# Pair 0 of x by SyncE alone: backward mirrored loads in the order of use, Q later, g_ln turned by TensorE

## Chip, cores and metric

The kernel runs on one core of a Trainium2 chip. The metric is the device time of one execution in microseconds. Before the change the median of three runs is 1128.04 us (1126.84 to 1128.88).

## What is computed

```python
X = np.fft.fft(x, axis=1)          # x: 8 x 3136 x 256, float32
X = np.fft.fft(X, axis=2)
t = X.real.reshape(25088, 256)
h = t @ w_in                       # 256 x 1024, float64
e = np.exp(h - h.max(-1))
s = h * e / (e.sum(-1) + 1e-09)
ln = (s - s.mean(-1)) / np.sqrt(s.var(-1) + 1e-06) * g_ln
out = ln @ w_out                   # 1024 x 256
```

The result is float32. The tables of the transforms (F, T, Q) and of row numbers (mirror) are inputs of the program.

## The kernel before

The batch is taken in four pairs of two images. In an image the 3136 rows are written as 49 x 64, n = 64 n1 + n2, so that a pair has 2 x 49 = 98 partitions, each with 64 rows of x. The real part of the transform needs rows n and -n only as a sum (features reversed too). Of the 64 columns, 32 are therefore loaded forward (`xa`, columns 1 to 32) and their mirror partners as `xb`; they come in NC = 8 chunks of CH = 4 rows (98 x 4096 bytes each). The mirror partners of the partitions of one image are its partitions in reverse, read from the last columns backward.

`load` (line 118) issues one chunk: `xa` from SyncE's queue (126), `xb` from GpSimd as an indirect DMA (128) whose row numbers are in `idx`, and with the last chunk `x0`, column 0. `add_mirror` (137) adds `xb` to `xa` in place, two VectorE instructions (143 and 145); `fold` (153) makes sums and differences of the features with lines 150, 151 and 163, into `y` (two buffers). `transform1` (185) multiplies a half chunk of `y` with F on TensorE (215), copies the result out on ScalarE (218), and `keep` (222) stores it to `zd` in DRAM (223), first only the 20 rows that the first group of frequencies needs. `turn` (225) reads `zd` back in another order for the second transform.

`Weights` (637) works beside this for pair 0. `w_in` comes as float64 bits in four pieces of 128 x 4096 bytes (`piece_in`, 581), and VectorE and ScalarE make float32 of them (`exponent_in`, `narrow_in`: lines 584 to 634). `Q` (664) is multiplied into the weights by `product_in` (685), `mid` (672) spreads one column of Q on ScalarE (676). `w_out` comes in two halves (700) and is made float32 and scaled by `g_ln` in `exponent_out` and `narrow_out`; `scale_out` (703) multiplies `g_ln` by 2**-20 first. `g_ln` is loaded by line 665 into 128 x 8, element by element.

The order of all this is written out by hand (`manual_schedule`, 784): each engine executes its instructions in the order in which they are written. SyncE's queue at the start is `idx`, w_in 0, w_in 1, xa 0, F, w_in 2, xa 1, w_in 3, xa 2, xa 3, Q, g_ln, xa 4, xa 5, then, as chunks are done, xa 6 and so on. The mirrored halves 0 to 5 stand on GpSimd at once. A SyncE DMA signals one of eight semaphores in turn, and its issue waits until the DMA eight places before it has landed. Chunks 2 to 5 lie in `room`, memory that is later `uT`; chunks 6 and 7 use the buffers of 0 and 1 again. For each chunk VectorE has: a piece of w_in (chunks 0 to 2), `add_mirror`, `fold`; after chunk 7 it goes on with w_out. In the turn of chunk 3, before its `transform1`, stand the loads of w_out and of T, `mid` and `scale_out`; after it `product_in(0)`.

From then on one unit (pair, k1) follows the other: second transform, products with w_in, softmax and statistics, products with w_out, store. Pairs 1 to 3 are loaded and folded beside the units, with GpSimd's indirect DMA for the mirrored half, and pair 0's outputs use `idx` too.

Of the kernel before, what the change touches and what calls it, by code (L numbers as in the profile page):

```python
# [9 lines left out]
FP32 = mybir.dt.float32  # L10
# [7 lines left out]
P = 128  # L18


N1, N2 = 49, 64
NK = N1 // 2 + 1
NH = N2 // 2
PR = 2 * N1
ZR = 4 * NK
CH = 4
NC = NH // CH
# [17 lines left out]
def kernel(  # L45
# [19 lines left out]
    nc = tc.nc  # L65
    B, S, D = x.shape
    FF = moe_w_in.shape[1]
    KF = FF // P
# [2 lines left out]
    HW = FF // 2  # L71

    x_g = x.rearrange("b (n1 g l) d -> (b n1 g) (l d)", n1=N1, l=CH)
    x_pn = x.rearrange("b (n1 n2) d -> (b n1) n2 d", n2=N2)
    out_k = out.rearrange("(p k2 k1) d -> p k1 k2 d", p=NP, k1=N1)

# [8 lines left out]
    fpool = ctx.enter_context(tc.tile_pool(name="fpool", bufs=2))  # L85
# [3 lines left out]
    F = const.tile([PR, 6, ZR], FP32, name="F")  # L89
# [6 lines left out]
    ident = const.tile([P, P], FP32, name="ident")  # L96
    neg_half = const.tile([P, 2], FP32, name="neg_half")
    idx = const.tile([P, NP * (NC + NK)], I32, name="idx")
    w_mid = const.tile([P, FF], FP32, name="w_mid")
    g_ln = const.tile([P, KF], FP32, name="g_ln")  # L100
# [5 lines left out]
    def result(i):  # L106

        return banks[i % 4]
# [9 lines left out]
    def load(pr, c, room=None):  # L118

        r = slice(pr.p * PR, (pr.p + 1) * PR)  # L120
        if room is None:
            xa = xpool.tile([PR, CH, D], FP32, tag="xa", name="xa")
            xb = xpool.tile([PR, CH, D], FP32, tag="xb", name="xb")
        else:
            xa, xb = (t.rearrange("p (l d) -> p l d", d=D) for t in room)
        nc.sync.dma_start(out=xa, in_=x_pn[r, c * CH + 1 : (c + 1) * CH + 1, :])
        i = pr.p * NC + c
        nc.gpsimd.indirect_dma_start(
            out=xb.rearrange("p l d -> p (l d)"), out_offset=None, in_=x_g,
            in_offset=bass.IndirectOffsetOnAxis(ap=idx[0:PR, i : i + 1], axis=0))  # L130
        x0 = None
        if c == NC - 1:
            x0 = xpool.tile([PR, 1, D], FP32, tag="x0", name="x0", bufs=1)
            nc.sync.dma_start(out=x0, in_=x_pn[r, 0:1, :])
        pr.raw[c] = (xa, xb, x0)

    def add_mirror(pr, c, engine, part=None):

        xa, xb, _ = pr.raw[c]
        rows = (0, CH) if part is None else (part * CH // 2, (part + 1) * CH // 2)  # L140
        r = slice(rows[0], min(rows[1], CH - 1 if c == NC - 1 else CH))
        a, rb = xa[:, r, :], xb[:, ::-1, :][:, r, :]
        i = engine.tensor_tensor(out=a[:, :, 1:D], in0=a[:, :, 1:D], in1=rb[:, :, D - 1 : 0 : -1], op=ALU.add)
        if part is None:
            engine.tensor_tensor(out=a[:, :, 0:1], in0=a[:, :, 0:1], in1=rb[:, :, 0:1], op=ALU.add)
        return i
# [6 lines left out]
    def fold(pr, c):  # L153

        xa, _, x0 = pr.raw.pop(c)
        pr.y[c] = xpool.tile([PR, CH, D], FP32, tag="y", name="y")
        sides = [(pr.y[c], xa)]
        if c == NC - 1:
            pr.y0 = xpool.tile([PR, 1, D], FP32, tag="y0", name="y0", bufs=1)
            sides.append((pr.y0, x0))  # L160
        for o, i in sides:
            fold_features(o, i)
            nc.vector.tensor_copy(out=o[:, :, 0:129:128], in_=i[:, :, 0:129:128])  # L163
# [21 lines left out]
    def transform1(pr, s):  # L185

        c, l = divmod(2 * s, CH)
        if s == 0:  # L190
            pr.zd = dram.tile([ZR, NH, D], FP32, tag="zd", name="zd")
        if l == 0:

            if pr.p or c < 2:
                pr.z = zpool.tile([ZR, CH, D], FP32, tag="z", name="z")
            elif c < 6:
                if c == 2:
                    pr.z_v = fpool.tile([P, 2, FF, 2], FP32, tag="v", name="z_v", bufs=2)
                pr.z = pr.z_v[0:ZR].rearrange("p a f b -> p (a f b)").rearrange("p (c l d) -> p c l d", c=4, l=CH)[:, c - 2]
            elif c == 6:  # L200
                pr.z = S_tiles[1][0:ZR, 0:2].rearrange("p a c k -> p (a c k)").rearrange("p (l d) -> p l d", l=CH)
            else:
                pr.z = gpool.tile([P, KG, D], FP32, tag="g", name="z_g")[0:ZR, 0:CH, :]
            pr.zs[c] = pr.z
        y = pr.y[c]
        ps = result(0 if pr.p else s).rearrange("p (l d) -> p l d", l=2)
        if s == NH // 2 - 1:
            parts = [(ps[0:ZR, 0], y[:, l], 0), (ps[0:ZR, 1], pr.y0[:, 0], 1), (ps[0:ZR, 1], y[:, l + 1], 2)]
        else:
            parts = [(ps[0:ZR], y[:, l : l + 2], 0)]  # L210
        pr.done.append(s)
        first = True
        for o, i, t in parts:
            for h, cs in enumerate((EVEN, ODD)):
                nc.tensor.matmul(o[..., cs], F[:, 2 * t + h, :], i[..., cs], start=first, stop=True,  # L215
                                 skip_group_check=True)
                first = False
        nc.scalar.copy(pr.z[:, l : l + 2, :], ps[0:ZR])
        if l == CH - 2:
            keep(pr, c, slice(0, ZR if pr.p else 4 * KG))  # L220
# [375 lines left out]
    def confine(unit, here=False, parts=(0, 1, 2)):  # L596

        if unit is None:
            return
        if here:  # L600
            bits(unit, unit, -896.0, ALU.add, 0.0, ALU.max)
            bits(unit, unit, 255.0, ALU.min, 2.0 ** 23, ALU.mult)
            return

        u = unit.bitcast(FP32)
        for i in parts:
            if i == 0:
                nc.scalar.activation(out=u, in_=unit, func=ACT.Relu, bias=limits[:, 0:1])
            elif i == 1:
                nc.scalar.activation(out=u, in_=u, func=ACT.Relu, bias=limits[:, 1:2], scale=-1.0)  # L610
            else:
                nc.scalar.activation(out=unit, in_=u, func=ACT.Identity, bias=limits[:, 2:3], scale=-(2.0 ** 23))
# [24 lines left out]
    class Weights:  # L637
# [24 lines left out]
        def load_tables(self):  # L662
            self.Q = fpool.tile([P, KD, D + 1], FP32, tag="ev", name="Q", bufs=1)
            nc.sync.dma_start(out=self.Q, in_=q_tab.rearrange("(c p) d -> p c d", p=P))
            nc.sync.dma_start(out=g_ln, in_=moe_g_ln.rearrange("(c p) -> p c", p=P))

        def load_table(self, i):
            k1 = slice(KG, NK) if i else slice(0, KG)
# [32 lines left out]
                                  in_=moe_w_out.bitcast(I32).rearrange("(c p) f -> p c f", p=P)[:, c])  # L701

        def scale_out(self):
            nc.scalar.mul(out=g_ln, in_=g_ln, mul=2.0 ** -20)

        def exponent_out(self, i):
            self.units.append(exponent(moe_w_out, self.raw[:, 2 * i * NW : 2 * (i + 1) * NW]))
# [76 lines left out]
    with tc.manual_schedule():  # L784
        pairs = [Pair(p) for p in range(NP)]
        first, weights = pairs[0], Weights()
        nc.sync.dma_start(out=idx, in_=mirror)
        make_identity(nc, ident)

        rooms = {}  # L790
# [2 lines left out]
            room = room[0:PR].rearrange("p w c i m -> p (w c i m)").rearrange("p (a n) -> p a n", a=4)  # L793
            rooms[c], rooms[c + 1] = [room[:, i] for i in (0, 1)], [room[:, i] for i in (2, 3)]
        weights.load_in()
        for c in range(4):
            weights.piece_in(c)
            if c:
                load(first, c - 1, rooms.get(c - 1))
            if c == 1:  # L800
                nc.sync.dma_start(out=F, in_=f_tab)
        load(first, 3, rooms[3])
        weights.load_tables()
        for c in range(4, 6):
            load(first, c, rooms[c])
        nc.vector.memset(ones, 1.0)
        nc.vector.memset(neg_half, -0.5)
        bits(top_bit, neg_half[:, 0:1].bitcast(I32), 31, ALU.logical_shift_right, 31, ALU.logical_shift_left)
# [6 lines left out]
        for c in range(NC):  # L815

            if c == 0:
                weights.narrow_in(0)
                weights.narrow_in(1)
            elif c < 3:  # L820
                weights.narrow_in(c + 1)
            if c < 2:
                weights.exponent_in(c + 2)
            add_mirror(first, c, nc.vector)
            fold(first, c)
            if c == NC - 1:
                for i in range(2):
                    weights.exponent_out(i)
                confine(weights.units[0], True)
                weights.narrow_out(0)  # L830
            if c + 6 < NC:
                load(first, c + 6)
            if c == 3:
                weights.place_out()
                for i in range(2):
                    weights.load_out(i)
                weights.load_table(0)
                weights.mid()
                weights.scale_out()
            for s in range(CH // 2):  # L840
                if c == NC - 1:
                    confine(weights.units[0], parts=(s,))
                transform1(first, c * CH // 2 + s)
            if c == 3:
                weights.keep_in(0, weights.product_in(0))
            elif c == 4:
                odd = weights.product_in(1, (0,))
            elif c == 5:
                weights.product_in(1, (1,), odd)
# [312 lines left out]
```

## Time and profile before

| | us |
|---|---|
| median of 3 runs | 1128.04 |
| the profiled execution | 1129.0 |
| its span | 1127.1 |
| PE busy | 1092.4 (97%) |
| DVE busy | 986.5 (88%) |
| ACT busy | 799.4 (71%) |
| POOL busy | 809.9 (72%) |
| SyncE's DMA queue, share of 16 engines | 63.7% |
| GpSimd's DMA queue, share of 16 engines | 13.3% |

Read it so: PE is TensorE's matmuls, DVE VectorE, ACT ScalarE, POOL GpSimd, SP SyncE. A busy time is summed over the span. In the page's strips each digit is the busy share, in tenths, of one fortieth of the span (28.2 us). A row of the timeline has the start, the duration, the engine, the line, the operation with its operands, and in brackets how long the engine stood idle before it and what ended that. An "SPq" row is the issue of a DMA and not its transfer. The trace also records the packets of the DMA engines with their size and duration, and each increment of a DMA semaphore: every DMA engine that takes part in a transfer posts one when its share has landed.

### The profile page before, as it was taken

The page shows a single profiled execution, that of the slowest core. Times are in us where ns is not written, and L with a number is a line of the kernel's source. Part 1 is how long each engine was busy: PE and PEld are TensorE (multiplying, and loading weights), DVE is VectorE, ACT ScalarE, POOL GpSimd, SP SyncE. Part 2 cuts the span into 40 slices and gives each one's busy share as a digit, 9 for nine tenths or more (in the row PEclk, how much of TensorE's full clock was granted, in tenths as well). Part 3 has the DMA queues.
Part 4 walks back from the last instruction along what each step waited for, and adds up shares of the span by engine and source line. Part 5 has one row for each costly group of instructions (what it writes and reads, how often), then busy time and mean ns, then how long its engine had stood idle before and what let it go on. Part 6 is the DMA issues. An engine that isn't in the chain of part 4 may idle for free. (4 is left out here: it accounts for less than half of the span.)

```text
span 1127.1 us, 21958 instructions
## 1 busy us (share of the span) xinstructions
PE 1092.4 (97%) x7030; PEld 873.9 (78%) x7030; DVE 986.5 (88%) x1440; ACT 799.4 (71%) x1946; POOL 809.9 (72%) x707
## 2 busy tenths in 40 slices
PE   2999999999999999999999999999999999999997
PEld 1657878878777787887887787887877788778887
DVE  7899898988889989898888989898888899898984
ACT  4579777777766877777767777777776777777761
POOL 3058888766896988775877788876686576766674
PEclk9899999999999999999999999999999999999999
DMA  9773897867897989976969797976779685965665
GB/s 239 215 198 85 179 198 189 175 151 152 152 196 154 194 178 193 183 154 142 169 151 184 169 194 177 203 176 150 154 147 169 131 164 116 162 141 114 140 136 120
DMA packets 458569, 185.77 MB, mean 165 GB/s; under 512 B 425774, under 2 KB 440374, under 8 KB 458456
## 3 DMA queue, kind: packets, MB, share of 16 engines
q1 hardware_dynamic: 444568, 145.96, 63.7%
q0 software_dynamic: 13888, 38.42, 13.3%
q8 instruction: 57, 0.93, 0.4%
q14 instruction: 56, 0.46, 0.1%
HBM read 44.78 MB, written 38.80 MB: 74 GB/s over the span
## 5 line engine op out<-in xcount | busy, mean ns | idle before, releaser
L279 PE MATMUL ps_h<-Wi,q 128*128 128x512 f32 x800 | 361.9, 593 | 2.2 <-DVE nmax L300 2.0
L455 POOL TENSOR_TENSOR S<-uT 128x512 f32<-128x512 f32 x186 | 238.5, 1282 | 111.0 <-DVE u L315 37.4
L462 PE MATMUL ps_m<-Ws,S 128*128 128x128 f32 x2304 | 296.3, 275 | 2.8 <-POOL rs L377 2.8
L462 PEld LDWEIGHTS ps_m<-Ws,S 128*128 128x128 f32 x2304 | 279.8, 192 | 6.3 <-POOL rs L377 2.9
L322 ACT ACTIVATE h<-u,usum 128x1024 f32<-128x1024 f32 x196 | 225.0, 1149 | 78.2 <-DVE u L315 76.9
L279 PEld LDWEIGHTS ps_h<-Wi,q 128*128 128x128 f32 x800 | 144.1, 190 | 147.1 <-issue 141.4
L315 DVE SCALAR_TENSOR_TENSOR u<-h,u 128x1024 f32<-128x1024 f32 x196 | 236.7, 1243 | 7.7 <-ACT u L308 7.7
L308 ACT ACTIVATE u<-h,nmax 128x1024 f32<-128x1024 f32 x196 | 223.4, 1141 | 4.6 <-DVE nmax L300 2.9
L386 DVE STREAM_TRANSPOSE v<-u 128x2048 f32<-128x2048 f32 x88 | 203.4, 2311 | 3.0
L462 PE MATMUL ps_m<-Wo,uT 128*128 128x128 f32 x1536 | 203.7, 276 | 1.0 <-DMA out_dram<-ot 1.0
L462 PEld LDWEIGHTS ps_m<-Wo,uT 128*128 128x128 f32 x1536 | 187.9, 192 | 2.1 <-issue 2.1
L549 POOL DMA_INDIRECT out_dram<-ot,idx x96 | 112.7, 1174 | 35.0 <-issue 12.6
L300 DVE CUSTOM_DVE_ANT_0 h<-ev,ps_h 128x1024 f32<-128x1024 f32 x100 | 122.1, 1221 | 17.4 <-DVE ev L292 9.0
L300 DVE CUSTOM_DVE_ANT_0 h<-h,ps_h 128x1024 f32<-128x1024 f32 x96 | 117.2, 1221 | 14.6 <-ACT ot L506 1.0
L292 DVE SCALAR_TENSOR_TENSOR ev<-w_mid,r,ps_h 128x1024 f32<-128x1024 f32 x99 | 122.9, 1241 | 1.4 <-PE ps_h L279 1.0
L455 POOL TENSOR_TENSOR S<-uT,S 128x512 f32<-128x512 f32 x93 | 118.9, 1279 | 7.2
L455 POOL TENSOR_TENSOR S<-S,uT 128x512 f32<-128x512 f32 x93 | 118.9, 1278 | 7.3
L462 PE MATMUL ps_m<-Ws,uT 128*128 128x128 f32 x768 | 101.8, 276 | 0.0
L462 PE MATMUL ps_m<-Wo,S 128*128 128x128 f32 x768 | 101.4, 275 | 0.0
L243 PEld LDWEIGHTS ps_m<-T,g 128*128 128x128 f32 x400 | 60.1, 191 | 47.3 <-issue 45.7
L215 PE MATMUL ps_m<-y,F 98*100 98x258 f32 (+3 forms) x288 | 72.0, 385 | 22.6 <-DVE y L163 22.6
L462 PEld LDWEIGHTS ps_m<-Ws,uT 128*128 128x128 f32 x768 | 93.8, 192 | 0.0
(109 smaller groups left out, 1186.6 us busy)
## 6 DMA issues: line engine op xcount, KB each, us to landing
uT<-v SPq DMA_DIRECT2D x752, 128.0 KB
g<-zd POOLq DMA_DIRECT2D x72, 160.0 KB, 5.4
out_dram<-ot SPq DMA_DIRECT2D x176, 64.0 KB
xa<-in_x_dram SPq DMA_DIRECT2D x28, 392.0 KB
zd<-z SPq DMA_DIRECT2D x24, 400.0 KB
raw_in<-in_moe_w_in_dram SPq DMA_DIRECT2D x4, 512.0 KB
raw_out<-in_moe_w_out_dram SPq DMA_DIRECT2D x2, 1024.0 KB
room<-in_x_dram SPq DMA_DIRECT2D x4, 392.0 KB
```

Of the source, the lines that this page charges most:

```text
L215: nc.tensor.matmul(o[..., cs], F[:, 2 * t + h, :], i[..., cs], start=first, stop=True, skip_group_check=True)
L243: nc.tensor.matmul(o, g[:, k, h * P : (h + 1) * P], table, start=(h == 0), stop=True, skip_group_check=True)
L279: nc.tensor.matmul(ps[:, fs], t.q[:, c * P : (c + 1) * P], Wi[:, c, fs], start=True, stop=not whole_even)
L292: nc.vector.scalar_tensor_tensor(out=t.ev, in0=w_mid, scalar=t.r, in1=ps, op0=ALU.mult, op1=ALU.add)
L300: nc.vector.tensor_tensor_reduce(out=t.h[s], in0=t.h[0] if s else t.ev, in1=t.odd, scale=1.0 if s else -0.5, scalar=3.0e38, op0=ALU.add, o ...
L308: nc.scalar.activation(out=t.u[s], in_=t.h[s], func=ACT.Exp, bias=t.nmax[:, s : s + 1], scale=-1.0, accum_out=t.esum[:, s : s + 1])
L315: t.last = nc.vector.scalar_tensor_tensor(out=t.u[s], in0=t.h[s], scalar=-1.0, in1=t.u[s], op0=ALU.mult, op1=ALU.mult, accum_out=t.usum[:, ...
L322: nc.scalar.activation(out=t.h[s], in_=t.u[s], func=ACT.Square, bias=t.usum[:, s : s + 1], scale=-float(FF), accum_out=t.ssq[:, s : s + 1])
L386: nc.vector.transpose(out=t.batch.v[:, :, t.w], in_=t.both.rearrange("p s (g n) -> p (s g) n", n=32))
L455: i = engine.tensor_tensor(out=S[j], in0=a, in1=b, op=op)
L462: nc.tensor.matmul(o, a[:, c], b[:, c], start=start and c == 0, stop=c == n - 1, skip_group_check=True)
L549: dma = nc.gpsimd.indirect_dma_start(out=out, out_offset=bass.IndirectOffsetOnAxis(ap=idx[:, i : i + 1], axis=0), in_=t.ot[s], in_offset=None)
```

## The change

The mirrored halves of pair 0 are issued by SyncE, behind the forward half of the same chunk, as a plain DMA whose source steps backward through the 49 rows of each of two images; the other pairs keep the indirect DMA. SyncE's queue at the start becomes w_in 0, w_in 1, chunk 0, F, g_ln, w_in 2, chunk 1, w_in 3, chunks 2 to 5, Q, idx. `g_ln` is loaded as 8 rows of 128 into a buffer of `ot1`, turned by TensorE into a PSUM bank in `scale_out`, and scaled from there. `mid` stands after chunk 3's `transform1`.

```diff
+    x_b = x.rearrange("b (n1 n2) d -> b n1 n2 d", n2=N2)
...
         nc.sync.dma_start(out=xa, in_=x_pn[r, c * CH + 1 : (c + 1) * CH + 1, :])
-        i = pr.p * NC + c
-        nc.gpsimd.indirect_dma_start(
-            out=xb.rearrange("p l d -> p (l d)"), out_offset=None, in_=x_g,
-            in_offset=bass.IndirectOffsetOnAxis(ap=idx[0:PR, i : i + 1], axis=0))
+        if pr.p == 0:
+            g = slice(S // N1 - (c + 1) * CH, S // N1 - c * CH)
+            nc.sync.dma_start(out=xb.rearrange("p l d -> p (l d)"), in_=x_b[0:2, ::-1, g, :].rearrange("b n l d -> b n (l d)"))
+        else:
+            i = pr.p * NC + c
+            nc.gpsimd.indirect_dma_start(
+                out=xb.rearrange("p l d -> p (l d)"), out_offset=None, in_=x_g,
+                in_offset=bass.IndirectOffsetOnAxis(ap=idx[0:PR, i : i + 1], axis=0))
...
         def load_tables(self):
             self.Q = fpool.tile([P, KD, D + 1], FP32, tag="ev", name="Q", bufs=1)
             nc.sync.dma_start(out=self.Q, in_=q_tab.rearrange("(c p) d -> p c d", p=P))
-            nc.sync.dma_start(out=g_ln, in_=moe_g_ln.rearrange("(c p) -> p c", p=P))
+
+        def load_gain(self):
+            self.gain = fpool.tile([P, D], FP32, tag="ot1", name="gain", bufs=3)[0:KF, 0:P]
+            nc.sync.dma_start(out=self.gain, in_=moe_g_ln.rearrange("(c p) -> c p", p=P))
...
         def scale_out(self):
-            nc.scalar.mul(out=g_ln, in_=g_ln, mul=2.0 ** -20)
+            ps = result(2)[:, 0:KF]
+            nc.tensor.matmul(ps, self.gain, ident[0:KF, 0:KF], is_transpose=True, start=True, stop=True)
+            nc.scalar.mul(out=g_ln, in_=ps, mul=2.0 ** -20)
...
-        nc.sync.dma_start(out=idx, in_=mirror)
...
-        for c in range(4):
-            weights.piece_in(c)
-            if c:
-                load(first, c - 1, rooms.get(c - 1))
-            if c == 1:
-                nc.sync.dma_start(out=F, in_=f_tab)
-        load(first, 3, rooms[3])
+        weights.piece_in(0)
+        weights.piece_in(1)
+        load(first, 0)
+        nc.sync.dma_start(out=F, in_=f_tab)
+        weights.load_gain()
+        weights.piece_in(2)
+        load(first, 1)
+        weights.piece_in(3)
+        for c in range(2, 6):
+            load(first, c, rooms[c])
         weights.load_tables()
-        for c in range(4, 6):
-            load(first, c, rooms[c])
+        nc.sync.dma_start(out=idx, in_=mirror)
...
-                weights.mid()
                 weights.scale_out()
...
             if c == 3:
+                weights.mid()
                 weights.keep_in(0, weights.product_in(0))
```

## Prediction

> **What bounds the kernel now.** I read the page first. Over the whole span PE is the limit, and only the first slices are not full:
>
> ```profile
> span 1127.1 us, 21958 instructions
> ...
> PE   2999999999999999999999999999999999999997
> ...
> DVE  7899898988889989898888989898888899898984
> ```
>
> The first slice (28.2 us) has PE at 2 tenths. All that the change touches runs in the first 60 us or so, so the question is how far the start moves; PE, busy 1040 of the 1051 us after 76 us, cannot give back a late start.
>
> Next, the table of windows over the start (columns: stretch, its length, busy us and instruction count of PE, PEld, DVE, ACT, POOL, clock, DMA share, GB/s):
>
> ```profile
> 0.00:14.60 14.60, 0.00 (x0) 0.00 (x0) 9.16 (x20) 5.50 (x7) 6.92 (x12) 1.00 0.87 244
> 14.60:22.00 7.40, 3.73 (x8) 2.15 (x8) 5.18 (x11) 3.34 (x5) 1.17 (x1) 1.00 1.05 252
> 22.00:35.60 13.60, 9.24 (x23) 6.12 (x24) 10.52 (x20) 5.61 (x11) 1.18 (x1) 0.62 0.95 207
> 35.60:46.30 10.70, 10.70 (x39) 6.52 (x38) 10.54 (x24) 4.61 (x8) 0.00 (x0) 1.00 0.96 321
> ```
>
> DMA is at 0.87 to 1.05 of 16 engines throughout, and DVE is busy 35.4 of 46.3 us. So the start is VectorE's chain (w_in pieces, then mirror-add and fold of eight chunks of x), fed by full DMA engines. The timeline tells which arrival ended each gap:
>
> ```profile
> 8.67 0.39 SPq L665 DMA_DIRECT2D g_ln<-in_moe_g_ln_dram  x1
> ...
> 10.49 16.96 SPq L126 DMA_DIRECT2D room<-in_x_dram  x2
> ...
> 14.27 0.43 DVE L584 TENSOR_SCALAR S<-raw_in 128x512 int32<-128x512 int32 x1 [2.01 <-DMA raw_in<-in_moe_w_in_dram]
> ...
> 35.65 1.22 DVE L143 TENSOR_TENSOR room<-room 98x1020 f32<-98x1020 f32 x1 [2.92 <-DMA room<-in_x_dram]
> ...
> 43.45 0.95 DVE L143 TENSOR_TENSOR xa<-xa,xb 98x765 f32<-98x765 f32 x1
> ...
> 46.26 0.75 DVE L584 TENSOR_SCALAR S<-raw_out 128x512 int32<-128x512 int32 x2
> ```
>
> One SP issue (room of chunk 4) hangs 16.5 us right behind g_ln's transfer. Chunk 7's mirror-add starts at 43.45, and at 46.26 VectorE goes on to w_out. I measure the change by when this instruction at 46.26 starts.
>
> **What the Trainium skill says.** (1) "DMA: Bandwidth & Descriptors", section "Why a DMA increments its semaphore by 16 and not by 1": the number of DMA engines that a transfer uses is the largest k up to 16 that divides the slowest non-1 dimension of both its source and its destination; a SyncE transfer takes the lowest-numbered k, and SyncE itself posts the missing increments at once. The trace agrees where both sides are alike: xa of chunk 0 (98 rows) has one increment at 2.70 us and then 14 between 7.62 and 8.65; zd of chunk 0 (20 rows) one at 28.54 and then 10 from 38.14 to 38.77. No transfer of the kernel before has unlike sides. (2) Same page, "Queues, rings and completion order": on one engine the descriptors of one queue are taken in order. The landings agree: w_in piece 0 from 4.14, piece 1 from 5.66, xa from 7.62, F from 8.75. (3) Same page, "Rules for kernel authors": a non-contiguous last dimension costs one descriptor per element. g_ln is that: 4 KB in pieces of 4 bytes, issued at 8.67, landed at 34.9.
>
> **The price of a row.** A chunk of x is 98 rows of 4096 B. Two windows of the DMA view bound one such packet on one engine (packets, MB, share of 16 engines). The first is 4 to 6 us, the second 33 to 36 us:
>
> ```profile
> q1 hardware_dynamic: 210, 0.74, 97.6%
> ```
>
> ```profile
> q1 hardware_dynamic: 201, 0.73, 87.4%
> ```
>
> 0.74 MB are 181 packets of 4 KB in 2 x 16 x 0.976 = 31.2 us: 172 ns each. 0.73 MB are 178 in 3 x 16 x 0.874 = 42.0 us: 236 ns each. The packet records give a median of 159 ns between 3 and 6 us, and that is the median of all xa loads issued alone later. With few engines active I take 165 ns, and keep 156 (the shortest seen) and 236 as ends.
>
> **The change, part by part.**
>
> *Mirrored rows on SP's queue.* Eight indirect issues on POOL (about 1.1 us each) go; POOL bounds nothing here, so 0. The replacement reads x with the dimensions [2, 49, 1024], the middle one backward, into [98, 1024]. The slowest dimensions are 2 and 98, so k = 2: two engines carry 49 rows each, where the indirect gather used all 16 (its landing counts show 16 increments) and xa uses 14. All SP transfers share the ring of engine 0, so I add up that ring in the new order, up to chunk 7's mirrored half: w_in 4 x 8 = 32 packets of 4 KB, xa 8 x 7 = 56, mirrored 8 x 49 = 392, together 480 x 0.165 = 79.2 us. Then F 7 x 0.144 = 1.0, Q 16 x 0.06 = 1.0 (its shorter ones), idx 8 x 0.028 = 0.2, zd of chunk 0 and the new g_ln rows 0.35. The ring starts at 1.9 us (first packet of idx in the trace), and I take 0.5 us for the last increment: chunk 7 is there at 1.9 + 81.75 + 0.5 = 84.1 us. SP keeps the ring fed: as built, each issue waits for the one eight places earlier, and among any eight stand three or more mirrored halves.
>
> VectorE then needs 46.26 - 43.45 = 2.8 us: 86.9. What is late next is w_out. Its first half is issued after xb of chunk 7; on engine 0 it stands behind x0 (7 x 0.05) and two zd stores (0.66) and takes 32 packets of 2 KB at 85 ns = 2.7 us: 1.9 + 81.75 + 3.7 + 0.5 = 87.9. So the instruction now at 46.26 starts at 87.9: **+41.6 us**. The second half follows 2.7 us later, within the 4.2 us that VectorE takes before it (46.26 to 50.45).
>
> *Chunk 7's chain to the second transform* keeps its length (fold, PE, copy, zd, turn); its zd store queues behind w_out's second half and T (32 x 0.085 + 8 x 0.055 = 3.2 us), and would land some 90.5 us, against 87.9 + 5 = 92.9 for the turn's old distance (51.28 - 46.26). Nothing added.
>
> *Q behind six chunks, mid() after chunk 3's transform.* On the same sum Q lands at about 65.5 us. ACT waits there in mid() (two instructions of 0.40), and PE in product_in(0); queued behind are chunk 4's transform and copies. Chunk 4's half lands at about 55 and chunk 5's at 64.5, so they wait up to 10 us, but y has two buffers and chunk 6 lands only at about 75: hidden by the same slow ring, 0. If the ring were quick, Q would come before chunk 3 is done, also 0.
>
> *g_ln in rows, turned by TensorE.* 1024 packets and the 16.5 us hang go. One transpose (L403's 128x128 form takes about 0.27 us) goes on PE, which is idle 4.4 of 13.6 us there, and ACT's scaling reads PSUM: 0, at most 0.5.
>
> *idx later.* It is first used by pair 1's loads on POOL, at 64.0 us now and some 105 then; it lands before 66: 0.
>
> Sum: the profiled execution, 1129.0 us around its span of 1127.1, becomes 1170.6; it lies 1.0 above the median 1128.04, so the median becomes about **1169 us**. With 156 ns it is 1165, with 236 ns 480 x 0.071 = 34 more, 1203.
>
> **Rivals.**
>
> *The split goes by the 98 rows, or over changing engines (faster).* For it: it is the shape of xa's own destination, which gets 14 engines, and no run here shows unlike sides. Then each engine has 7 rows per half, chunk 0 lies in by about 8 us, chunk 5 by 23, and VectorE is never starved: w_in work to about 12, chunk 0 until 15, two more pieces and chunk 1 until 22.4, six chunks of 2.78 until 39.1. The instruction now at 46.26 starts 7.2 us earlier: 1121 us. The deciding point: chunk 7 must land by 43.4, so 8 x 98/k packets have to fit into (43.4 - 4.9)/0.165 - 88 = 145, k of at least 5.4. The divisors 7 and 14 win, 2 loses.
>
> *One engine.* If the backward dimension confines it further: 32 + 56 + 784 = 872 packets, 64.7 us more: 1234 us. Against it: both sides are divisible by 2.
>
> *No net change.* Six or so engines in effect, so that the gain at chunks 0 to 3 is lost at chunks 6 and 7: 1128 us. No divisor gives it; only a mixed rate would.
>
> **How the numbers follow.** Two engines 0.82; the wide split 0.12; no net change 0.03; one engine 0.03. The range takes in the two-engine case from early catching-up (1155) to the slow packet (1204) and leaves out the others, 0.18, and little of its own. Both signs do not share the weight, so no second range is needed. Faster by over 0.2% (about what a measurement of this kernel can tell from no change) 0.12, within 0.2% 0.03, slower by over 0.2% 0.85.
>
> **What would show it.** Right: VectorE waits on a DMA before each mirror-add, about 9 us apart from chunk 2 on (56 x 0.165), the DMA share in the first 80 us falls to some four tenths, chunk 7's add near 84 us, and a mirrored transfer shows two late increments. Packet price wrong: the same picture at another pitch. Wrong altogether: seven or fourteen late increments, and chunk 7's add before 43 us.

## The result and the profile after

| | before | after |
|---|---|---|
| median, us | 1128.46 (1126.84 to 1131.05, 6 runs) | 1173.50 (1172.46 to 1174.10, 6 runs) |
| the profiled execution, us | 1129.0 | 1174.1 |
| its span, us | 1127.1 | 1172.3 |

The ratio is 1.0401, with a 95% interval of 1.0386 to 1.0415: 45 us slower, where 41 were forecast. The page of the kernel after shows where on the span they lie:

```profile
span 1172.3 us, 21951 instructions
...
PE   1348999999999999999999999999999999999998
...
DVE  4328998898888998988888999889898999899893
```

A slice is now 29.3 us. PE begins with 1, 3, 4 and 8 tenths, where before it had 2 and then 9, and DVE is at 4, 3 and 2 tenths in the first three slices. After them the strips are nearly as before. The table of windows gives the start (columns as before: PE, PEld, DVE, ACT, POOL, clock, DMA share, GB/s; the clock column reads 1.00 where the trace has no record of the clock, and the first record here is at 72.57 us, so it says nothing in these rows):

```profile
0.00:14.60 14.60, 0.00 (x0) 0.00 (x0) 8.68 (x19) 5.50 (x7) 0.69 (x6) 1.00 0.64 189
14.60:22.00 7.40, 0.00 (x0) 0.00 (x0) 1.60 (x4) 1.11 (x2) 0.00 (x0) 1.00 0.50 152
22.00:35.60 13.60, 5.89 (x13) 3.72 (x14) 8.84 (x18) 4.49 (x8) 0.00 (x0) 1.00 0.26 86
35.60:46.30 10.70, 4.97 (x12) 2.72 (x10) 2.90 (x6) 1.66 (x3) 0.00 (x0) 1.00 0.29 101
46.30:60.00 13.70, 4.22 (x10) 2.33 (x9) 4.59 (x9) 1.84 (x4) 0.00 (x0) 1.00 0.30 95
```

In the first four of these stretches the DMA share was 0.87 to 1.05 before. It is now 0.64 and 0.50, and 0.26 to 0.30 from 22 us on. So the cause isn't too much traffic: most of the DMA engines stand idle while the compute engines wait. The DMA view of 40 to 50 us (packets, MB, share of 16 engines) says how many work:

```profile
q1 hardware_dynamic: 137, 0.52, 13.1%
```

Two engines of sixteen, always busy, would be 12.5%. The timeline of VectorE names what it waits for:

```profile
20.39 0.43 DVE L589 TENSOR_SCALAR S<-raw_in 128x512 int32<-128x512 int32 x1 [8.96 <-DMA raw_in<-in_moe_w_in_dram]
...
40.06 1.22 DVE L148 TENSOR_TENSOR room<-room 98x1020 f32<-98x1020 f32 x1 [4.24 <-DMA room<-in_x_dram]
48.96 1.22 DVE L148 TENSOR_TENSOR room<-room 98x1020 f32<-98x1020 f32 x1 [6.20 <-DMA room<-in_x_dram]
...
88.34 0.95 DVE L148 TENSOR_TENSOR xa<-xa,xb 98x765 f32<-98x765 f32 x1 [8.15 <-DMA xb<-in_x_dram]
91.86 0.76 DVE L589 TENSOR_SCALAR S<-raw_out 128x512 int32<-128x512 int32 x2 [0.62 <-DMA raw_out<-in_moe_w_out_dram]
```

Before each mirror-add from chunk 2 on there is a wait of 4 to 8 us, and the adds start 8.9 to 10.8 us apart. The first row shows that the ring, the line of packets that wait on one DMA engine, is shared: it is a piece of w_in that VectorE waits for. Fourteen engines had posted for it between 8.39 and 10.96 us, and the last two at 19.98 and 20.36, because on those two it stood behind chunk 0's mirrored half. The instruction that started at 46.26 us starts at 91.86: +45.6 us, and the profiled time is +45.1.

The increments of the DMA semaphores show the two engines themselves. Each mirrored half has one increment at its issue and then exactly two (us):

```
chunk          0      1      2      3      4      5      6      7
first of two  17.18  28.82  39.51  48.40  57.66  67.28  77.02  88.16
second        17.53  29.14  39.97  48.86  57.95  67.80  77.40  88.31
```

### The profile page after: what moved, and what is told of

It is laid out like the page before. It is cut to its first block, busy times and chain, and to the rows that moved or that the text cites. A ratio compares the mean times of both kernels' runs of the same rounds, so it can differ in the third digit from the quotient of the medians.

```text
span 1172.3 us, 21951 instructions
## 1 busy us (share of the span) xinstructions
PE 1099.5 (94%) x7031; PEld 877.0 (75%) x7031; DVE 986.1 (84%) x1440; ACT 799.4 (68%) x1946; POOL 801.5 (68%) x699
## 3 DMA queue, kind: packets, MB, share of 16 engines
q1 hardware_dynamic: 444344, 149.17, 61.2%
## 5 line engine op out<-in xcount | busy, mean ns | idle before, releaser
L305 DVE CUSTOM_DVE_ANT_0 h<-h,ps_h 128x1024 f32<-128x1024 f32 x96 | 117.2, 1221 | 14.6 <-ACT ot L511 1.0
L220 PE MATMUL ps_m<-y,F 98*100 98x258 f32 (+3 forms) x288 | 75.9, 401 | 50.0 <-DVE y L168 50.0
L236 POOL DMA_DIRECT2D g<-zd x76 | 45.8, 612 | 97.5 <-DMA zd<-z_g 97.4
```

The source lines that it names most:

```text
L305: nc.vector.tensor_tensor_reduce(out=t.h[s], in0=t.h[0] if s else t.ev, in1=t.odd, scale=1.0 if s else -0.5, scalar=3.0e38, op0=ALU.add, o ...
```

## Experiments

**Theory:** the outermost dimension of the source, the two images, confines each mirrored half to two engines, always the same ones, and everything that SyncE issues queues there. **Rivals:** stepping backward is what is slow; or the cost is in the other parts of the change (order, Q, g_ln). Ratios are against the kernel before on the same chip, with the 95% interval. Diffs are against the changed kernel unless the text says otherwise. In `forward_two`, `backward_14`, `backward_7`, `one_engine` and `backward_14_turn_late` pair 0 adds other rows than the reference's; the bytes are the same.

### Number of engines: two forward, fourteen, seven, one

`forward_two`: the same two images as the outer dimension, but forward.

```diff
-x_b[0:2, ::-1, g, :]
+x_b[0:3:2, :, g, :]
```

> The mirrored halves of pair 0 are read forward, from images 0 and 2, in place of backward from images 0 and 1: the dimensions stay [2, 49, 1024], nothing steps backward, and pair 0's sums are of other rows. Theory (the slowest dimension of 2 puts a transfer on two engines): nothing changes, 1173.5 us, 1170 to 1177, two late increments for each mirrored half. Rival (reading backward is what is slow): the start is no longer held up and the time falls to about 1121 us.

Measured: 1174.57 us, ratio 1.0407 (1.0381 to 1.0433), again two late increments for each half and chunk 7 in at 87.87. Going backward costs nothing here.

`backward_14` and `backward_7`: backward in groups, so that the outer dimension is 14 (shown) or 7.

```diff
+rows = x_pn[r, g, :].rearrange("(a i) l d -> a i (l d)", a=14)
+nc.sync.dma_start(out=xb.rearrange("p l d -> p (l d)"), in_=rows[:, ::-1])
```

> The mirrored halves are read backward within 14 groups of seven rows, so that the dimensions are [14, 7, 1024] in place of [2, 49, 1024] and the same rows and bytes are moved; pair 0's sums pair other rows. Theory: 14 engines with seven rows each, 14 late increments, VectorE no longer waits on x, and the time is that of the wide split in the prediction, 1121 us (1117 to 1126). Rival (backward is slow): still about 1173 us.

> As the run with 14 groups, but with seven groups of 14 rows, [7, 14, 1024]; pair 0's sums pair other rows. Theory: seven engines, seven late increments; one engine's ring holds 32 + 56 + 8 x 14 = 200 packets, chunk 7 there at about 40 us, so 1123 us (1119 to 1128). Rival (what counts is not the number of engines but the place in the queue or the direction): about 1173 us.

Measured: 1125.68, ratio 0.9961 (0.9950 to 0.9973), with 14 late increments and chunk 7 in at 35.9 us; and 1129.78, ratio 1.0009 (0.9995 to 1.0023), with 7 late increments and chunk 7 in at 48.8. So with everything else of the change kept, the number of engines alone moves the time from 1173.5 to 1125.7. But fourteen came out at the slow end of what was expected, and seven missed it: 1129.8 for 1119 to 1128. Two timelines of VectorE tell why. The first is `backward_14`:

```profile
34.52 0.69 DVE L156 TENSOR_TENSOR y<-room 98x508 f32<-98x508 f32 x1 [1.92 <-PE ps_m L221]
39.68 0.69 DVE L156 TENSOR_TENSOR y<-xa 98x508 f32<-98x508 f32 x1 [2.59 <-PE ps_m L221]
...
44.02 0.76 DVE L590 TENSOR_SCALAR S<-raw_out 128x512 int32<-128x512 int32 x2
```

There x is early, and the releaser is now PE: VectorE waits for TensorE to free a buffer of `y`. The second is `backward_7`, where x is still what it mostly waits for, up to the end:

```profile
43.60 1.22 DVE L149 TENSOR_TENSOR xa<-xa,xb 98x1020 f32<-98x1020 f32 x1 [3.78 <-DMA xb<-in_x_dram]
...
52.51 0.77 DVE L590 TENSOR_SCALAR S<-raw_out 128x512 int32<-128x512 int32 x2 [0.80 <-DMA raw_out<-in_moe_w_out_dram]
```

For seven engines I had put chunk 7 at about 40 us, with a price per packet near that for few engines, and it came at 48.8. Between 6 and 21 us of this trace a 4 KB packet has a median of 248 ns.

`one_engine`: each half as 97 rows and one row; 97 is prime, so 1 is the only divisor up to 16.

```diff
+for a, z in ((0, PR - 1), (PR - 1, PR)):
+    nc.sync.dma_start(out=xb[a:z], in_=x_pn[a:z, g, :])
```

> The changed kernel, with each mirrored half of pair 0 as a forward transfer of 97 rows and one of a single row, so that pair 0 adds other rows than the reference's. Theory (the number of engines is the largest that divides the slowest dimensions, 97 is prime, so one engine carries it): one late increment, 8 x 49 more packets on engine 0 at 0.16 us, 63 us more than the changed kernel: about 1236 (1228 to 1250). Rival (the cost lies in the two-image view and not in the number of engines): about 1128, with an arrival as of the forward halves.

Measured: 1235.18 us (ratio 1.0947, 1.0932 to 1.0963), 61.7 more than the changed kernel. VectorE's timeline of `one_engine`:

```profile
95.97 1.22 DVE L149 TENSOR_TENSOR room<-room 98x1020 f32<-98x1020 f32 x1 [14.61 <-DMA room<-in_x_dram]
112.98 1.22 DVE L149 TENSOR_TENSOR room<-room 98x1020 f32<-98x1020 f32 x1 [14.32 <-DMA room<-in_x_dram]
...
153.09 0.76 DVE L590 TENSOR_SCALAR S<-raw_out 128x512 int32<-128x512 int32 x2 [0.60 <-DMA raw_out<-in_moe_w_out_dram]
```

The pitch is 17.0 us for 98 + 7 packets, 162 ns each, and the first w_out instruction is 61.2 us later than in the changed kernel, which for 392 packets is 156 ns each. With 49 and with 98 rows per engine the time follows the sum of one ring at some 160 ns a packet. With 14 rows, where more engines work and a packet costs more, that sum is too short.

### The same transfers from another queue

`mirror_gpsimd`: the unchanged backward transfers, issued by GpSimd; `mirror_gpsimd_turn_late`: with g_ln's turn also put after product_in(0).

```diff
-nc.sync.dma_start(out=xb.rearrange("p l d -> p (l d)"), in_=x_b[0:2, ::-1, g, :].rearrange("b n l d -> b n (l d)"))
+nc.gpsimd.dma_start(out=xb.rearrange("p l d -> p (l d)"), in_=x_b[0:2, ::-1, g, :].rearrange("b n l d -> b n (l d)"))
```

> The changed kernel with one edit: the same backward transfers of pair 0, issued from GpSimd's queue in place of SyncE's. Theory (two engines per transfer, and the harm is that all eight mirrored halves queue on the same two; the Trainium skill, DMA: Bandwidth & Descriptors, section Why a DMA increments its semaphore by 16 and not by 1, says that transfers issued by GpSimd take k consecutive engines from a cursor that moves on): each half again shows two data increments and takes some 8 to 10 us, but the eight halves lie side by side on different pairs of engines, so that chunk 5 is in before 30 us and chunk 7 before 43: about 1126 (1122 to 1130), with g_ln's turn still ahead of chunk 3. Rival (the two engines stay the same, or a half's own 8 to 10 us is what VectorE waits for): 1150 to 1174.

> The same with g_ln's turn and scaling after product_in(0). Theory of the gap on TensorE: chunk 3 is done 1.2 to 2.3 us earlier (the difference seen in the two pairs of traces so far), so 1 to 2 us less than mirror_gpsimd: about 1124.5. Rival (VectorE is held by something else next): no difference between the two.

Measured: 1147.22 us, ratio 1.0159 (1.0136 to 1.0183), and 1144.17, ratio 1.0124 (1.0105 to 1.0143). The expected 1126 was missed by 21 us. The halves do lie side by side: six of them land between 30.7 and 40.2 us, and in the stretch of 21 to 39 us GpSimd's queue fills 74.4% of 16 engines, which two could not. The increments show it too. Each half posts sixteen, and those that come after 29 us are 2, 4, 6, 8, 10 and 12 for halves 0 to 5: so it looks when each half has its rows on two engines that the halves before it did not use, as expected. But the halves come late. `mirror_gpsimd`, the DMA view of 6 to 21 us:

```profile
q1 hardware_dynamic: 1084, 3.28, 84.0%
q0 software_dynamic: 1506, 0.35, 16.1%
```

and VectorE's timeline of the same kernel:

```profile
30.69 1.22 DVE L148 TENSOR_TENSOR xa<-xa,xb 98x1020 f32<-98x1020 f32 x1 [14.61 <-DMA xb<-in_x_dram]
```

SyncE's loads, chunks 1 to 5 among them, moved 3.28 MB while GpSimd's moved 0.35, though the latter were issued from 1.6 us on; chunk 0's half landed at 30.67. It is this one late half that VectorE waits 14.6 us for. The packet records suggest why. Of GpSimd's 1506 packets only 85 are rows of 4 KB, and 1421 are of 4 bytes. Over the eight halves there are 784 rows and 5616 packets of 4 bytes, which is 8 x (14 x 49 + 16), as if each engine without rows of a half got a 4-byte packet for each of 49 rows, and every engine one for its increment. The two engines with chunk 0's half begin on its rows at 7.46 us and end by 30.67, at 0.47 us a row for 49 rows. That is about one packet of GpSimd and one of SyncE in turn (medians of 238 and 244 ns in this stretch). This is a reading of the records; no run tests it.

Of the 45 us, 26 come back when the halves don't all share two engines; the first w_out instruction, at 62.08, is 15.8 us late, about what chunk 0's half costs.

### The rest of the change alone

`indirect_kept`: all of the change but its first part, so the indirect loads stay and `idx` is first in the queue again.

```diff
-        if pr.p == 0:
-            g = slice(S // N1 - (c + 1) * CH, S // N1 - c * CH)
-            nc.sync.dma_start(out=xb.rearrange("p l d -> p (l d)"), in_=x_b[0:2, ::-1, g, :].rearrange("b n l d -> b n (l d)"))
-        else:
...
+        nc.sync.dma_start(out=idx, in_=mirror)
         make_identity(nc, ident)
```

> The change without its first part: the mirrored halves stay GpSimd's indirect loads (idx is loaded first again), with the new order of SyncE's queue, Q behind six chunks, g_ln in rows turned by TensorE and mid() later. Theory: the whole loss is in the mirrored loads, and the rest helps, since chunks come in the order of use and g_ln's 1024 pieces are gone: about 1123 us (1119 to 1127). Rival (a later Q, mid() or the turned g_ln costs time too): 1130 us or more.

Measured: 1133.17, ratio 1.0037 (1.0018 to 1.0056). This missed, and with the other sign: I had costed these parts at nothing. Some of it is arrivals (the last w_in piece at 26.57 us where it was 21.85). A second part showed in TensorE's timeline, around the turn of g_ln. To see it alone I put only that on the kernel before, in its old place (`gain_early`) and after product_in(0) (`gain_only`). Against the kernel before, without the move of `scale_out` in `gain_only`:

```diff
-            nc.sync.dma_start(out=g_ln, in_=moe_g_ln.rearrange("(c p) -> p c", p=P))
+            self.gain = fpool.tile([P, D], FP32, tag="ot1", name="gain", bufs=3)[0:KF, 0:P]
+            nc.sync.dma_start(out=self.gain, in_=moe_g_ln.rearrange("(c p) -> c p", p=P))
...
-            nc.scalar.mul(out=g_ln, in_=g_ln, mul=2.0 ** -20)
+            ps = result(2)[:, 0:KF]
+            nc.tensor.matmul(ps, self.gain, ident[0:KF, 0:KF], is_transpose=True, start=True, stop=True)
+            nc.scalar.mul(out=g_ln, in_=ps, mul=2.0 ** -20)
```

> The kernel before with one part of the change alone: g_ln loaded as 8 rows in its old place in the queue and turned by TensorE in the old place of scale_out, ahead of chunk 3's matmuls. The run with the turn after product_in(0) had 1128.1 and the ratio 0.9998. Theory of the gap: 1.2 to 2.3 us more, about 1129.8, ratio 1.001 to 1.002, chunk 3's matmuls in 3.7 us. Rival (the turn is hidden): 1128, ratio 1.000.

> The kernel before with one part of the change alone: g_ln loaded as 8 rows in its old place in the queue and turned by TensorE after product_in(0). Theory (the element-wise load of g_ln, 1024 packets, held SyncE for 16.5 us and so chunk 4's forward half, for which VectorE waited 2.92 us): the hang and that wait vanish, about 1126.5. Rival (the mirrored half or TensorE ends the same gap): 1129, unchanged.

Measured: 1131.87, ratio 1.0022 (1.0010 to 1.0035), and 1128.08, ratio 0.9998 (0.9985 to 1.0011). TensorE's timeline of `gain_early`:

```profile
31.07 3.71 PE L215 MATMUL ps_m<-y,F 98*100 98x258 f32 x8 [1.34 <-DVE y L163]
34.70 0.27 PE L706 MATMUL ps_m<-ident,gain 8*128 8x8 f32 x1
36.10 3.74 PE L215 MATMUL ps_m<-y,F 98*100 98x258 f32 x8 [1.13 <-ACT g_ln L707]
39.63 4.75 PE L686 MATMUL wps<-w_in,Q 128*128 128x512 f32 x8
44.22 1.89 PE L215 MATMUL ps_m<-y,F 98*100 98x258 f32 x8
```

and of `gain_only`:

```profile
31.03 6.41 PE L215 MATMUL ps_m<-y,F 98*100 98x258 f32 x16 [1.34 <-DVE y L163]
37.27 3.60 PE L686 MATMUL wps<-w_in,Q 128*128 128x512 f32 x8
40.80 0.22 PE L706 MATMUL ps_m<-ident,gain 8*128 8x8 f32 x1
40.95 1.97 PE L215 MATMUL ps_m<-y,F 98*100 98x258 f32 x8
```

The turn writes the PSUM bank of the chunk's next result, so TensorE stands until ScalarE has scaled out of it, here 1.13 us, as `mid` is ahead on ScalarE. Chunk 2 starts at the same time in both, and chunk 4's matmuls 3.3 us later with the early turn. Turn and gap are 1.4 of it. The rest is mostly pace: chunk 3's matmuls and the product with Q after them take 8.1 us here (36.10 to 44.22) and 6.3 in `gain_only` (34.52 to 40.80). The Trainium skill, "TensorE: Matmul & The Clock Gate", section "Part 1: The HAM clock gate (the "warmup" mystery)", says that TensorE runs at half clock until about 3.4 us of sustained work, within a free-running window. The traces agree: eight matmuls take 3.7 us from the first chunk on and 1.9 once chunk has followed chunk without a gap, and the first record of the full clock is at 41.93 us in `gain_early` and at 36.58 in `gain_only`. How much of these 5.4 us is the gap's doing, and how much the place of the window, two single traces do not show.

Two more kernels carry the late turn: `indirect_turn_late` and `backward_14_turn_late`, each with the one edit

```diff
-                weights.scale_out()
             for s in range(CH // 2):
...
                 weights.keep_in(0, weights.product_in(0))
+                weights.scale_out()
```

> The kernel with the indirect mirrored loads kept (1133.2 us), with one edit: g_ln's turn and scaling on TensorE and ScalarE stand after product_in(0) and no longer ahead of chunk 3's eight matmuls. Theory (the turn leaves a gap of about 0.6 us on TensorE ahead of that chunk, which keeps it at half clock for eight more matmuls, some 2.5 us in all, handed to VectorE through y's two buffers): about 1130.7, chunk 3's matmuls in 1.9 us instead of 3.7. Rival (the 4 us come from x, w_in and F arriving later in the new order alone): 1133, unchanged.

> The fourteen-engine split (1125.7 us), with g_ln's turn after product_in(0). Its mirrored rows run backward only within groups of seven, so pair 0 adds other rows than the reference's. Theory of the cold TensorE: 2 to 3 us less, about 1123.2, and VectorE's waits on TensorE before the folds of chunks 5 and 6 (4.5 us together) fall by about that. Rival (VectorE is held by something else next, such as w_out's first half): 1125.7, unchanged.

Measured: 1129.51, ratio 1.0016 (1.0006 to 1.0027), against 1.0037 with the early turn; and 1123.72, ratio 0.9965 (0.9952 to 0.9978), against 0.9961. With `mirror_gpsimd` (1.0159 to 1.0124) that makes four pairs. The late turn is better by 0.21, 0.24 and 0.35% in three of them, each hardly more than its uncertainty, and by nothing in `backward_14`, though its trace has the first unit 1.2 us earlier (55.85 for 57.04). In the profiled run of `mirror_gpsimd` the full clock is on record from 49.72 us, before chunk 3, which was quick even after the gap (1.97 us). So there the trace does not show what the times do. I take the turn at some 2 us where TensorE is the next bound: the delay is shown in the trace of `gain_early`, its size is uncertain. The 1.8 us by which `indirect_turn_late` is still slower than the kernel before stay open between the order of the loads and the scatter of arrivals.

`gain_only` tests a second reading of mine. SyncE's 16.96 us hang behind g_ln's transfer is down to 4.22 in it. Its timelines of SyncE's issues and of VectorE:

```profile
12.52 4.22 SPq L126 DMA_DIRECT2D room<-in_x_dram  x2
...
35.94 1.22 DVE L143 TENSOR_TENSOR room<-room 98x1020 f32<-98x1020 f32 x1 [2.47 <-DMA room<-in_x_dram]
```

The wait for chunk 4 is still there (2.92 before), and chunk 4's forward half lands at 35.84 us for 35.55, although SyncE is through with the issues of chunks 4 and 5 by 16.7 us, for 27.5: the engines were full without g_ln's pieces too. So the hang cost nothing that can be measured.

Last, `gain_q_late`: `gain_only` with Q behind chunks 4 and 5 and `mid` after chunk 3's transform.

```diff
-        load(first, 3, rooms[3])
-        weights.load_tables()
-        for c in range(4, 6):
+        for c in range(3, 6):
             load(first, c, rooms[c])
+        weights.load_tables()
...
-                weights.mid()
...
             if c == 3:
+                weights.mid()
```

> The kernel with g_ln in rows and the late turn (1128.1, ratio 0.9998), with Q's load moved behind chunks 4 and 5 and mid() behind chunk 3's transform: all parts of the change that do no harm by themselves, on the old order of w_in and x and with the indirect loads. Theory (the start is bound by the bytes of full DMA engines; Q is 0.26 MB, some 1.1 us at the 252 GB/s of the start): chunk 4's forward half comes about a microsecond earlier, VectorE's wait of 2.5 us for it shrinks to about 1.4, about 1127, ratio 0.999. Rival (TensorE then waits for Q in product_in(0) and gives it back, or other transfers take the room): 1128, ratio 1.000 or a little more.

Measured: 1128.83, ratio 1.0002 (0.9989 to 1.0016), the rival's number. VectorE's timeline of `gain_q_late`:

```profile
22.29 0.43 DVE L584 TENSOR_SCALAR S<-raw_in 128x512 int32<-128x512 int32 x1 [1.42 <-DMA raw_in<-in_moe_w_in_dram]
42.19 0.69 DVE L150 TENSOR_TENSOR y<-xa 98x508 f32<-98x508 f32 x1 [2.73 <-PE ps_m L215]
```

Between these two the wait for chunk 4 has gone, and a wait of 2.73 us on TensorE stands in its place; TensorE itself had waited 0.52 us for Q at 36.40. No version with the reference's mirrored rows beat the kernel before.

## Why the prediction was right, and where it was off

*Two engines for each mirrored half: right.* Two increments, a DMA share of 13.1%, and the runs with one, two, seven and fourteen engines follow the rule of the Trainium skill, "DMA: Bandwidth & Descriptors", "Why a DMA increments its semaphore by 16 and not by 1". With two, seven and fourteen they do so where source and destination differ, which no transfer of the kernel before had shown. One reading beside it does not hold: that the indirect loads post sixteen increments does not show that sixteen engines carry their rows, for in `mirror_gpsimd` the halves post sixteen too, with their rows on two engines each, as it seems.

*The sum over engine 0's ring: right in form, its price mis-sized.* Chunk 7's half was to land at 84.1 us and came at 88.2. The term that failed is the price of a packet, 165 ns, for the first 72 packets, up to chunk 0's half. By the forecast's own sum, with its 0.5 us for the last increment, this half was due at 14.3 us; it came at 17.2, which is (17.2 - 0.5 - 1.9) / 72 = 206 ns a packet and 2.9 us too late. In that stretch the other engines still worked (a DMA share of 0.64 and 0.50). After it the price held: with 2.5 us for the small transfers, the 408 packets from 17.2 to 88.2 us took 168 ns each, 1.2 us more in all. "With few engines active" was the condition I gave for 165 ns, and it did not hold at the start; my own upper row, 236 ns, was for full engines.

*What is late next: right.* W_out's first half ends the wait, 0.62 us of it, and VectorE starts on it 3.7 us after chunk 7's half, as the sum had it (87.9 - 84.1 = 3.8).

*Chunk 7's chain keeps its length: nearly.* The first unit's instruction on VectorE is at 106.06 us for 58.59, 47.5 later, 1.9 more than w_out's. TensorE is at half clock for chunk 7, on record from 86.22 to 96.46 us: the 16 matmuls take 4.56 us at 90.92. None of these 1.9 us can be seen in the end: from this instruction to the end of the span there are 1068.5 us before and 1066.2 after, and 1064.8 to 1068.5 in the fourteen traces of this study. Two microseconds of a single profile are within that scatter.

*Q and mid() hidden: right.* Q landed at 68.4 us (forecast 65.5). TensorE's timeline of the kernel after:

```profile
46.54 0.27 PE L713 MATMUL ps_m<-ident,gain 8*128 8x8 f32 x1
51.80 3.70 PE L220 MATMUL ps_m<-y,F 98*100 98x258 f32 x8 [4.99 <-DVE y L168]
68.45 5.73 PE L693 MATMUL wps<-w_in,Q 128*128 128x512 f32 x8 [12.94 <-DMA Q<-in_q_tab_dram]
...
90.92 4.56 PE L220 MATMUL ps_m<-y,F 98*100 98x258 f32 x16 [8.63 <-DVE y L168]
```

A wait of 12.94 us for Q looks bad, but it is given back: at 80.34 us TensorE has caught up and waits 0.99 us for `y`, and before chunk 7 it waits 8.63 us for `y` all the same.

*g_ln's turn, 0 and at most 0.5: mis-sized as a term, harmless in this kernel.* Here it hides in a wait of 4.99 us for `y`. Where x comes quickly it cost some 2 us or more in three pairs of four, since I had costed the transpose alone and neither the wait for ScalarE in its bank nor the clock. And the step "1024 packets and the 16.5 us hang go" was no gain to count on: the hang was SyncE's, not VectorE's.

*The faster rival, 1121 us.* Tried with fourteen engines it gives 1125.7, a ratio of 0.9961, and with the late turn 0.9965. Its step "VectorE is never starved" overlooked TensorE, which is next: w_out started at 44.02, not at 39.1. Seven engines, on the winning side of my deciding point (5.4), gave 1129.8, no gain: the point is about seven, since it was worked out with 165 ns and the packets cost more when seven engines work. With one engine, 1234 was worked out and 1235.2 measured. That is closer than the sum deserves: it started from 1169, 4.5 too low, and its step of 64.7 was 3.0 too long (61.7 measured), so two errors cancel.

## What to carry over

Before a transfer is reshaped, look at the slowest dimension of both its sides: it sets how many DMA engines carry it, and here the narrow transfers from SyncE all used the same ones, so that a narrow transfer also delays every wide one issued after it. Add up the one ring that all of them share, packet by packet; that sum gave the time within 4 us in 45 where one or two engines set the pace. Removing a wait at a start that several things bound (bytes, VectorE, TensorE) mostly shows the next one: check which that is before counting the gain.

## What was not expected of the hardware

- A 4 KB packet's price went with how many engines were at work: a median of 214.5 ns between 6 and 21 us of the changed kernel, 159 when two are active (21 to 39 us).
- With both queues full of work, GpSimd's plain transfers on two engines each moved 0.35 MB in 15 us beside SyncE's 3.28 MB, with 85 packets of 4 KB and 1421 of 4 bytes. The kernel before's indirect loads, in the same stretch, had 423 packets of 4 KB and 115 of 4 bytes, to SyncE's 474 of 4 KB.
- In five of these traces (`backward_14`, `backward_7`, `indirect_kept`, `gain_early`, `mirror_gpsimd`) a gap of 0.55 to 1.13 us on TensorE, behind the turn of g_ln, lies ahead of chunk 3. In four of them the next eight matmuls take 3.7 us, in `mirror_gpsimd` 1.97.
